# Attention, Fourier mixing and feed-forward on one core: third group's P halves in a weight slot, and VectorE's score operations ordered behind a feed-forward eviction

## The chip, the core and the metric

The kernel runs on one core of a Trainium2 chip. Its engines are TensorE (PE; its weight loads are listed as PEld), VectorE (DVE), ScalarE (ACT), GpSimd (POOL) and SyncE (SP), each with its own instruction stream; they meet only by semaphores. The metric is the device time of one execution in microseconds. Each run gives one time; of several, the median is used.

## What is computed

Eight batches of 576 positions with eight heads of 64 go through causal attention with a window of 128 and a linear bias, then through a two-dimensional Fourier mixing with a residual and a layer norm, then through a feed-forward layer of 512 to 2048 to 512 with a second residual:

```python
scores = np.matmul(q, k.transpose(0, 1, 3, 2)) / np.sqrt(D)
scores = np.where(mask, scores + bias[None], -1e9)      # 0 <= rel < 128
attn = softmax(scores)                                  # exp, sum, divide
x = np.matmul(attn, v).transpose(0, 2, 1, 3).reshape(B, S, H * D)
...
u = x + np.real(np.fft.fft(np.fft.fft(x, axis=1), axis=2))
un = (u - mean(u)) / np.sqrt(var(u) + 1e-06)
return u + np.maximum(un @ w_ch1, 0.0) @ w_ch2
```

Arrays are float32. The kernel multiplies in float16, with most operands split into a high and a low half, so that each product is made of three.

## The kernel before

**Three kinds of work.** Attention goes by pairs of heads, p = 0 to 31, four pairs a batch, two heads e = 0, 1 in each. The transform (`fourier`) and the layer norm of a batch follow its four pairs. The feed-forward (`ffn`) of a batch comes after that: L863 multiplies the first layer into a PSUM tile `fp`, of which there are two; ACT evicts its rectified high half into `hbuf` (L868), and DVE then writes the low half (the lambda behind L868, recorded as L166); L877 multiplies the second layer, again into `fp`, and DVE adds it to X (`X<-fp`, L166). The three kinds run interleaved: while one batch is in attention, earlier ones are in the transform and the feed-forward, so that PE has matmuls of one kind while another waits.

**Attention of pairs 8 to 31.** Each pair's scores come in three groups i = 0, 1, 2, of 384, 512 and 256 columns for each head. PE writes the scores into PSUM tiles `sp`. On DVE `biased` (L456) adds the bias, writes P in float32 and its minimum to `nb`; on ACT the exponential runs in place (`P<-P,nb`, L166). Then `halves` splits P: ACT writes the high half in float16 (L467) and DVE the low half (`P<-P`, L166), both into a second tile, `both`. `flip` (L474) has SP start a transposing DMA of it into `pt`, and PE multiplies `pt` with the values (`pv`, L506, L509, L510).

**Buffers.** The float32 P of `biased` and the halves come from one pool of four buffers named P, for each head one. Which buffer an allocation gets is settled as the program is built. In most groups the halves get the buffers that held the halves of the group before, so ACT's L467 waits there until the transposes that read these have landed; the float32 P mostly gets the other two. `wall` are two constant tiles that hold the feed-forward's weights in nine slots of 1024; half of slot 8 of the second one holds only a small block of zeros at the start.

**What sets the order.** A planner runs pieces of work from a heap by due time: `put(t, f)` for a time, `after(dt, f)` for a delay after the present piece. Groups are numbered n = 3(p - 8) + i; the scores of an even and the following odd n are issued together by `both`, then `biased` of the first group, and `biased` of the second one at its own due time. What the planner emits is then ordered again, engine by engine, by a list scheduler that goes by dependences and buffers; so a new dependence, or another buffer, can move instructions on every engine. Each engine runs its list in order.

**L151** sums squares of q, k and v over the partitions (`total`, `pd<-sq`) for the scales of a later pair; ACT writes these squares at L285.

Of the kernel before, what the change touches and what calls it, by code (L numbers as in the profile page):

```python
# [3 lines left out]

# [6 lines left out]
F32 = mybir.dt.float32  # L11
F16 = mybir.dt.float16
# [4 lines left out]
ALU = mybir.AluOpType  # L17
# [6 lines left out]
NF = 2  # L24
# [11 lines left out]
PB = 4  # L36
# [40 lines left out]
def attn_fft_ffn_kernel(  # L77
# [15 lines left out]
    nc = tc.nc  # L93
    B = q.shape[0]
    V, A, G, T = nc.vector, nc.scalar, nc.gpsimd, nc.tensor
    PSUM = bass.MemoryType.PSUM

    def pool(name, bufs, **kw):
        return ctx.enter_context(tc.tile_pool(name=name, bufs=bufs, **kw))

    const, xp, att = pool("const", 1), pool("xp", 3), pool("att", 2)
# [29 lines left out]
    wall = [const.tile([128, 9, 1024], F32, name=f"wall{i}") for i in range(2)]  # L131
    wf = [t.bitcast(F16).rearrange("p s (e x) -> p s e x", e=2) for t in wall]

    zeros = wall[1][:, 8, 512:576].bitcast(F16)
    G.memset(zeros, 0.0)
    G.memset(wall[1][:, 0], 0.0)

# [27 lines left out]
    def after(dt, f, *a, **kw):  # L165
        put(now[0] + dt, lambda: f(*a, **kw))  # L166
# [3 lines left out]
    behind, marks = [None], {}  # L170
# [272 lines left out]
    def biased(p, i):  # L443
        b, j = divmod(p, 4)
        sp, grp = banks.pop((p, i)), SGRP[i]
        P = Ps[p, i] = {}
        for e in range(2):
            h = 2 * j + e
            nb = small.tile([128, 5], F32, name="nb", bufs=6)
            col = 0  # L450
            whole = P[e] = att.tile([128, 512], F32, name="P", bufs=PB)
            for ti in grp:
                m, n, pc = TILES[ti][1], 128 * len(TILES[ti][2]), PCOL[ti]
                pt = P[e, ti] = whole[:, col:col + n]
                tab, mul = (rel_sb, -2.0 ** -(h + 1)) if b < NF else (psc[p][2], psc[p][1][:m, e:e + 1])
                V.tensor_tensor_reduce(pt[:m, 0:n], sp[e][:m, col:col + n], tab[:m, pc:pc + n],  # L456
                                       mul, 3.0e38, ALU.add, ALU.min, nb[:m, ti:ti + 1])
                after(0.25, A.activation, pt[:m, 0:n], pt[:m, 0:n], AF.Exp, bias=nb[:m, ti:ti + 1], scale=-1.0)
                col += n
            if b >= NF:  # L460
                after(0.45, halves, p, i, e, col)

    def halves(p, i, e, n):
        P32 = Ps[p, i][e][:, 0:n]
        both = att.tile([128, 512], F32, name="P", bufs=PB).bitcast(F16)
        hi, lo = both[:, 0:n], both[:, n:2 * n]
        A.activation(hi, P32, AF.Copy, scale=2.0 ** 14)  # L467
        after(0.2, V.scalar_tensor_tensor, lo, P32, 2.0 ** 14, hi, ALU.mult, ALU.subtract)
        after(0.4, flip, p, i, e, both[:, 0:2 * n])
# [377 lines left out]

    ov = out.rearrange("(t p) d -> t p d", p=128)

    def ffn(b):  # L850
        X = Xs[b]
        parts = [(uTs[b][i], 256, [X[:, XS[2 * i]], X[:, XS[2 * i + 1]]], 4 * b + 2 * i) for i in range(2)]
        if b % 2 == 1:
            parts.append((uTs[b][2], 128, [uts[b // 2]], 4 * B + b // 2))
        for uT, n, tiles, slot in parts:
            per = 512 // n
            hh = []
            for f0 in range(0, 16, per):
                fp = ps_f.tile([128, 512], F32, name="fp")
                for i in range(per):  # L860
                    for c in range(4):
                        for p, (e, j) in enumerate(((0, 0), (0, 1), (1, 0))):
                            T.matmul(fp[:, i * n:(i + 1) * n], w1_ap(e, c, f0 + i), uT[:, j, c, 0:n],  # L863
                                     start=(c == 0 and p == 0), stop=(c == 3 and p == 2))
                    if i == per // 2 - 1:
                        yield
                ht = next(hslots)
                A.activation(ht[:, 0], fp, AF.Relu)  # L868
                after(0.2, V.scalar_tensor_tensor, ht[:, 1], fp, 0.0, ht[:, 0], ALU.max, ALU.subtract)
                for i in range(per):  # L870
                    hh.append(ht[:, :, i * n:(i + 1) * n])
                yield
            for i, t in enumerate(tiles):
                op = ps_f.tile([128, 512], F32, name="fp")
                for f in range(16):
                    for p, (a, e) in enumerate(((0, 0), (0, 1), (1, 0))):
                        T.matmul(op, hh[f][:, a, i * 128:(i + 1) * 128], w2_ap(e, f),  # L877
                                 start=(f == 0 and p == 0), stop=(f == 15 and p == 2))
                    if f % 2 == 1 and f < 15:
                        yield  # L880
                after(0.15, V.scalar_tensor_tensor, t, op, wone, t, ALU.mult, ALU.add)
                after(0.4, nc.sync.dma_start, out=ov[slot + i], in_=t)
                yield
# [4 lines left out]
    for p in range(4 * B):  # L888
        b, j = divmod(p, 4)
# [26 lines left out]
        for i in range(3):  # L916
# [3 lines left out]
            n = 3 * (p - 4 * NF) + i  # L920
# [19 lines left out]
    for b in range(B):  # L940
        t = begin_of(4 * b)
        fourier(b, transform_of(b))
        n = 80 if b % 2 else 64
# [10 lines left out]
    while queue:  # L954
# [6 lines left out]
        for i in fresh:  # L961
            e = i.engine
# [125 lines left out]
```

## Time and profile before

| | us |
|---|---|
| median of three runs | 1046.98 (1043.87 to 1048.29) |
| the profiled execution, its own time | 1043.62 |
| span of its trace | 1041.8 |
| PE busy in the span | 1011.7 |
| DVE busy | 707.2 |
| ACT busy | 551.1 |

The profile lists for every instruction its start, its duration and, in brackets, how long its engine had been idle before it and what ended that idle time. L numbers are lines of the kernel before; L166 is the helper that runs delayed pieces, so several operations of DVE and ACT carry it and are told apart by their tiles. Consecutive matmuls are shown as one row with a count. The granted clock is given as a share of TensorE's full speed.

### The profile page before, as it was taken

The page shows a single profiled execution, that of the slowest core. Times are in us where ns is not written, and L with a number is a line of the kernel's source. Part 1 is how long each engine was busy: PE and PEld are TensorE (multiplying, and loading weights), DVE is VectorE, ACT ScalarE, POOL GpSimd, SP SyncE. Part 2 cuts the span into 40 slices and gives each one's busy share as a digit, 9 for nine tenths or more (in the row PEclk, how much of TensorE's full clock was granted, in tenths as well). Part 3 has the DMA queues.
Part 4 walks back from the last instruction along what each step waited for, and adds up shares of the span by engine and source line. Part 5 has one row for each costly group of instructions (what it writes and reads, how often), then busy time and mean ns, then how long its engine had stood idle before and what let it go on. Part 6 is the DMA issues. An engine that isn't in the chain of part 4 may idle for free.

```text
span 1041.8 us, 23224 instructions
## 1 busy us (share of the span) xinstructions
PE 1011.7 (97%) x9201; PEld 732.2 (70%) x9201; DVE 707.2 (68%) x2124; ACT 551.1 (53%) x1217; POOL 24.2 (2%) x68
## 2 busy tenths in 40 slices
PE   7999999989999999998999999999999999999998
PEld 6978967657676675856585685867586775857756
DVE  5899895977577869796678768698577735351111
ACT  7887865675445755775455654576445521331100
POOL 0000000100000000000000000000000000000000
PEclk9999999999999999999999999999999999999999
DMA  9955223385434543445343543446332510030000
GB/s 359 346 181 163 53 57 95 64 164 110 83 58 98 118 99 81 95 103 117 70 82 70 114 94 69 98 93 143 72 76 45 84 42 11 11 71 2 21 11 21
DMA packets 179789, 97.51 MB, mean 94 GB/s; under 512 B 153952, under 2 KB 162144, under 8 KB 179680
## 3 DMA queue, kind: packets, MB, share of 16 engines
q1 hardware_dynamic: 179392, 95.72, 38.4%
q8 instruction: 72, 1.18, 0.5%
q14 instruction: 37, 0.30, 0.1%
q10 hardware_dynamic: 288, 0.30, 0.1%
HBM read 49.33 MB, written 9.44 MB: 56 GB/s over the span
## 4 chain that ended last, share of the span: by engine, by line
PE 75%; DVE 12%; ACT 5%; DMA 5%; issue 3%; SPq 0%; POOL 0%; ACTq 0%; DVEq 0%; POOLq 0%
PE fp L877 30%; PE fp L863 27%; DMA pt<-P 4%; PE pd L621 3%; PE sp L425 3%; PE sp L427 3%; PE pv L500 3%; DVE P L456 1%; PE sp L483 1%; DVE hbuf L166 1%; ACT P L166 1%; DVE P L166 1%; PE pv L506 1%; PE pd L683 1%; PE pv L509 1%
## 5 line engine op out<-in xcount | busy, mean ns | idle before, releaser
L877 PE MATMUL fp<-wall,hbuf 128*128 128x512 f16 x1728 | 391.3, 379 | 0.1
L863 PEld LDWEIGHTS <-wall 128*128 128x128 f16 x3840 | 340.1, 98 | 57.5 <-issue 12.7
L863 PE MATMUL fp<-uT,wall 128*128 128x256 f16 x3072 | 361.2, 273 | 11.2 <-DVE sc L267 5.2
L877 PEld LDWEIGHTS <-hbuf 128*128 128x128 f16 x1728 | 163.7, 98 | 183.3 <-issue 3.4
L166 ACT ACTIVATE P<-P,nb 128x256 f32<-128x256 f32 x320 | 140.1, 478 | 99.6 <-DVE nb L456 97.5
L868 ACT ACTIVATE hbuf<-fp 128x512 f16<-128x512 f32 x144 | 84.9, 589 | 157.2 <-PE fp L863 157.1
L166 DVE SCALAR_TENSOR_TENSOR hbuf<-fp,hbuf 128x512 f16<-128x512 f32 x144 | 98.9, 688 | 99.8 <-ACT hbuf L868 99.4
L456 DVE CUSTOM_DVE_ANT_0 P<-sp,rg,nsl 128x256 f32<-128x256 f32 x240 | 98.5, 451 | 32.1 <-PE sp L427 29.2
L166 DVE SCALAR_TENSOR_TENSOR P<-P 128x384 f16<-128x384 f32 (+1 forms) x144 | 78.1, 552 | 52.8 <-ACT P L467 52.5
L467 ACT ACTIVATE P<-P 128x384 f16<-128x384 f32 (+1 forms) x144 | 71.8, 515 | 46.3 <-DMA pt<-P 41.8
L166 DVE SCALAR_TENSOR_TENSOR X<-fp,misc,X 128x512 f32<-128x512 f32 x32 | 23.7, 739 | 47.4 <-PE fp L877 47.3
L506 PE MATMUL pv<-vhs,pt 128*128 128x65 f16 x432 | 53.5, 195 | 0.8 <-DVE X L525 0.6
L509 PE MATMUL pv<-vl,pt 128*128 128x64 f16 x432 | 53.5, 193 | 0.0
L510 PE MATMUL pv<-vhs,pt 128*128 128x65 f16 x432 | 53.4, 193 | 0.0
L863 PE MATMUL fp<-wall,wall 128*128 128x128 f16 x768 | 45.8, 219 | 3.3 <-DVE hbuf L166 2.8
L506 PEld LDWEIGHTS <-pt 128*128 128x128 f16 x432 | 41.0, 98 | 8.9 <-issue 1.4
L509 PEld LDWEIGHTS <-pt 128*128 128x128 f16 x432 | 40.3, 99 | 7.4 <-issue 0.2
L427 PE MATMUL sp<-kk,qq 64*128 64x256 f16 x720 | 42.7, 260 | 0.0
L510 PEld LDWEIGHTS <-pt 128*128 128x128 f16 x432 | 40.7, 98 | 0.0
L604 ACT ACTIVATE fh<-abcd,sc 128x512 f16<-128x512 f32 (+1 forms) x21 | 15.1, 719 | 47.9 <-DVE abcd L592 33.2
L427 PEld LDWEIGHTS <-qq 64*128 64x128 f16 x720 | 30.1, 94 | 12.1 <-issue 8.4
L621 PE MATMUL pd<-tab_sb,fh 128*128 128x289 f16 x168 | 37.2, 287 | 0.0
(208 smaller groups left out, 1239.4 us busy)
## 6 DMA issues: line engine op xcount, KB each, us to landing
qr<-q_dram SPq DMA_DIRECT2D x28, 304.0 KB, 3.3
out_dram<-X SPq DMA_DIRECT2D x32, 256.0 KB, 2.3
hbuf<-w_dram SPq DMA_DIRECT2D x16, 511.8 KB, 7.7
vr<-v_dram SPq DMA_DIRECT2D x23, 320.0 KB, 3.1
kr<-k_dram SPq DMA_DIRECT2D x24, 289.0 KB, 2.9
X<-w_dram SPq DMA_DIRECT2D x11, 511.8 KB, 4.0
uT<-w_dram SPq DMA_DIRECT2D x5, 511.8 KB, 4.7
pt<-P SPq DMA_TRANSPOSE x144, 2.9
```

The costliest lines, as they stand in the source:

```text
L166: put(now[0] + dt, lambda: f(*a, **kw))
L425: T.matmul(sp[e][:m, col:col + n], lhs, keys(kk, ti), start=True, stop=True)
L427: o = T.matmul(sp[e][:m, col:col + n], qq[h, c0:c0 + m], keys(kk[h], ti), start=(x == 0), stop=(x == len(prods) - 1))
L456: V.tensor_tensor_reduce(pt[:m, 0:n], sp[e][:m, col:col + n], tab[:m, pc:pc + n], mul, 3.0e38, ALU.add, ALU.min, nb[:m, ti:ti + 1])
L467: A.activation(hi, P32, AF.Copy, scale=2.0 ** 14)
L506: o = T.matmul(pv[:, ti], ph, vh[:, e, vc], start=first, stop=False)
L509: T.matmul(pv[:, ti, 0:D], ph, vl[:, e, vc], start=False, stop=False)
L510: T.matmul(pv[:, ti], pl, vh[:, e, vc], start=False, stop=last)
L621: T.matmul(zp[:, :NS], st["in", c][l][:m, g], tab1_sb[:m, (0 if g < 2 else 2) + t, c], start=(c == 0 and p == 0), stop=(c == 2 and p == 2))
L863: T.matmul(fp[:, i * n:(i + 1) * n], w1_ap(e, c, f0 + i), uT[:, j, c, 0:n], start=(c == 0 and p == 0), stop=(c == 3 and p == 2))
L868: A.activation(ht[:, 0], fp, AF.Relu)
L877: T.matmul(op, hh[f][:, a, i * 128:(i + 1) * 128], w2_ap(e, f), start=(f == 0 and p == 0), stop=(f == 15 and p == 2))
```

## The change

For the third group of a pair (i = 2) `halves` no longer takes a buffer from the pool P, but the second half of slot 8 of the second weight tile, 512 float16 columns for each head. The first and second groups go on taking theirs from the pool. And the first operation of `biased` for a second group (odd n, first head, first tile) now has an order dependence on `marks["fed"]`, the last low-half eviction of the feed-forward's first layer that was emitted before it; a named function, `lower_half`, replaces the lambda, to note that instruction.

```diff
@@ -1,4 +1,4 @@
-from contextlib import ExitStack
+from contextlib import ExitStack, nullcontext
 from heapq import heappop, heappush
 from itertools import count, cycle
 
@@ -132,6 +132,7 @@
     wf = [t.bitcast(F16).rearrange("p s (e x) -> p s e x", e=2) for t in wall]
 
     zeros = wall[1][:, 8, 512:576].bitcast(F16)
+    last_half = wall[1][:, 8, 512:1024].bitcast(F16)
     G.memset(zeros, 0.0)
     G.memset(wall[1][:, 0], 0.0)
 
@@ -453,8 +454,9 @@
                 m, n, pc = TILES[ti][1], 128 * len(TILES[ti][2]), PCOL[ti]
                 pt = P[e, ti] = whole[:, col:col + n]
                 tab, mul = (rel_sb, -2.0 ** -(h + 1)) if b < NF else (psc[p][2], psc[p][1][:m, e:e + 1])
-                V.tensor_tensor_reduce(pt[:m, 0:n], sp[e][:m, col:col + n], tab[:m, pc:pc + n],
-                                       mul, 3.0e38, ALU.add, ALU.min, nb[:m, ti:ti + 1])
+                with tc.issue_after(marks["fed"]) if b >= NF and (3 * p + i) % 2 and e + col == 0 else nullcontext():
+                    V.tensor_tensor_reduce(pt[:m, 0:n], sp[e][:m, col:col + n], tab[:m, pc:pc + n],
+                                           mul, 3.0e38, ALU.add, ALU.min, nb[:m, ti:ti + 1])
                 after(0.25, A.activation, pt[:m, 0:n], pt[:m, 0:n], AF.Exp, bias=nb[:m, ti:ti + 1], scale=-1.0)
                 col += n
             if b >= NF:
@@ -462,7 +464,10 @@
 
     def halves(p, i, e, n):
         P32 = Ps[p, i][e][:, 0:n]
-        both = att.tile([128, 512], F32, name="P", bufs=PB).bitcast(F16)
+        if i == 2:
+            both = last_half[:, 512 * e:512 * e + 512]
+        else:
+            both = att.tile([128, 512], F32, name="P", bufs=PB).bitcast(F16)
         hi, lo = both[:, 0:n], both[:, n:2 * n]
         A.activation(hi, P32, AF.Copy, scale=2.0 ** 14)
         after(0.2, V.scalar_tensor_tensor, lo, P32, 2.0 ** 14, hi, ALU.mult, ALU.subtract)
@@ -847,6 +852,10 @@
 
     ov = out.rearrange("(t p) d -> t p d", p=128)
 
+    def lower_half(ht, fp):
+        V.scalar_tensor_tensor(ht[:, 1], fp, 0.0, ht[:, 0], ALU.max, ALU.subtract)
+        marks["fed"] = nc.cur_bb.bb.instructions[-1]
+
     def ffn(b):
         X = Xs[b]
         parts = [(uTs[b][i], 256, [X[:, XS[2 * i]], X[:, XS[2 * i + 1]]], 4 * b + 2 * i) for i in range(2)]
@@ -866,7 +875,7 @@
                         yield
                 ht = next(hslots)
                 A.activation(ht[:, 0], fp, AF.Relu)
-                after(0.2, V.scalar_tensor_tensor, ht[:, 1], fp, 0.0, ht[:, 0], ALU.max, ALU.subtract)
+                after(0.2, lower_half, ht, fp)
                 for i in range(per):
                     hh.append(ht[:, :, i * n:(i + 1) * n])
                 yield
```

No instruction is added or taken away on the engines; the order of some is other, and so are buffers and waits. In the changed program line numbers are higher: L456 is L458, L467 is L472, L474 is L479, L868 is L877, the low-half eviction is L856 (before: L166), the other delayed pieces are L167, L525 is L530.

On ACT, at the end of pair 19 (470 to 478 us in the trace of before), these are the exponentials, the halves (`P<-P` without `nb`) and the high-half evictions before,

```order
L467 ACTIVATE P<-P 128x512 x2
L166 ACTIVATE P<-P,nb 128x256 x2
L467 ACTIVATE P<-P 128x256
L868 ACTIVATE hbuf<-fp 128x512
L467 ACTIVATE P<-P 128x256
L396 ACTIVATE vhs<-vr,psc 128x10x64
L868 ACTIVATE hbuf<-fp 128x512
```

and after:

```order
L472 ACTIVATE P<-P 128x512 x2
L167 ACTIVATE P<-P,nb 128x256 x2
L472 ACTIVATE wall_106<-P 128x256 x2
L877 ACTIVATE hbuf<-fp 128x512
L397 ACTIVATE vhs<-vr,psc 128x10x64
L877 ACTIVATE hbuf<-fp 128x512
```

The two halves of the third group now write `wall_106` and stand together ahead of the eviction that stood between them.

On DVE, in pair 20 (490 to 498 us), where the second group's scores are first read (ISA is the operation of L456, with a second entry for its minimum; the numbers behind `sp` only tell score tiles apart), before:

```order
L166 SCALAR_TENSOR_TENSOR P<-P 128x384
L456 ISA P,nb<-sp_7099,rg,nsl 128x256
L456 ISA nb 128x1
L456 ISA P,nb<-sp_7099,rg,nsl 128x256
L456 ISA nb 128x1
L166 SCALAR_TENSOR_TENSOR hbuf<-fp,hbuf 128x512
L166 SCALAR_TENSOR_TENSOR P<-P 128x384
L456 ISA P,nb<-sp_7100,rg,nsl 128x256
```

and after:

```order
L167 SCALAR_TENSOR_TENSOR P<-P 128x384
L856 SCALAR_TENSOR_TENSOR hbuf<-fp,hbuf 128x512
L167 SCALAR_TENSOR_TENSOR P<-P 128x384
L856 SCALAR_TENSOR_TENSOR hbuf<-fp,hbuf 128x512
L528 TENSOR_SCALAR ri<-pv,psc 128x5
L529 RECIPROCAL ri<-ri 128x5
L530 TENSOR_TENSOR X<-pv,ri 128x5x64
L856 SCALAR_TENSOR_TENSOR hbuf<-fp,hbuf 128x512
L458 ISA P,nb<-sp_7075,rg,nsl 128x256
L458 ISA nb 128x1
```

The operations of the second group (L456 before, L458 after) moved from ahead of the first of three `hbuf` evictions to behind the third, and behind `ri` and `X<-pv` of pair 19 as well.

On DVE, between pairs 10 and 11 (223 to 228 us), before:

```order
L523 TENSOR_SCALAR ri<-pv,psc 128x5
L524 RECIPROCAL ri<-ri 128x5
L166 SCALAR_TENSOR_TENSOR vl<-vr,psc,vhs 128x640
L525 TENSOR_TENSOR X<-pv,ri 128x5x64
L166 SCALAR_TENSOR_TENSOR X<-fp,misc,X 128x512
L166 SCALAR_TENSOR_TENSOR P<-P 128x256 x2
L456 ISA P,nb<-sp_3022,rg,nsl 128x256
```

and after:

```order
L458 ISA P,nb<-sp_3018,rg,nsl 128x256
L458 ISA nb 128x1
L458 ISA P,nb<-sp_3018,rg,nsl 128x128
L458 ISA nb 128x1
L529 RECIPROCAL ri<-ri 128x5
L167 SCALAR_TENSOR_TENSOR vl<-vr,psc,vhs 128x640
L458 ISA P,nb<-sp_3019,rg,nsl 128x256
L458 ISA nb 128x1
L458 ISA P,nb<-sp_3019,rg,nsl 128x128
L458 ISA nb 128x1
L530 TENSOR_TENSOR X<-pv,ri 128x5x64
L167 SCALAR_TENSOR_TENSOR X<-fp,misc,X 128x512
```

Here the score operations of pair 11 (`sp_3022` and `sp_3023` before, `sp_3018` and `sp_3019` after) moved from behind `X<-fp` and the third group's low halves of pair 10 to ahead of them. In the changed program the P that they write lies in the buffers of the halves of pair 10's second group, and they wait for the transposes of these.

## Rows read from the trace of the kernel before

**Rows 1.** Page, part 1: engine busy us (share of the span) xinstructions

```profile
PE 1011.7 (97%) x9201; PEld 732.2 (70%) x9201; DVE 707.2 (68%) x2124; ACT 551.1 (53%) x1217; POOL 24.2 (2%) x68
```

**Rows 2.** Idle time by releaser: engine line <- releaser: us, times, longest

```profile
ACT P L467 <- DMA pt<-P: 41.8, 29, 3.4
...
PE fp L863 <- DVE hbuf L166: 7.4, 10, 1.9
...
PE fp L863 <- DVE sc L267: 5.2, 2, 3.4
...
PE pd L151 <- ACT wall L285: 3.1, 1, 3.1
...
DVE P L456 <- DMA pt<-P: 2.4, 3, 1.0
...
PE pv L506 <- DVE X L525: 0.6, 1, 0.6
```

**Rows 3.** Groups by line and shape: xcount | busy, mean ns | idle before

```profile
L467 ACT ACTIVATE P<-P 128x512 f16<-128x512 f32 x48 | 29.8, 624 | 14.2 <-DMA pt<-P 13.6
...
L467 ACT ACTIVATE P<-P 128x256 f16<-128x256 f32 x48 | 18.6, 409 | 28.9 <-DMA pt<-P 25.1 <-DVE P L166 2.4 <-DVE nmr L830 1.2
```

**Rows 4.** ACT's timeline, 475 to 477: start, duration (us), instruction [idle before <-releaser]

```profile
475.82 0.42 ACT L467 ACTIVATE P<-P 128x256 f16<-128x256 f32 x1 [3.40 <-DMA pt<-P]
476.14 0.58 ACT L868 ACTIVATE hbuf<-fp 128x512 f16<-128x512 f32 x1
```

**Rows 5.** Timeline of DVE, 476 to 478

```profile
476.27 0.43 DVE L166 SCALAR_TENSOR_TENSOR P<-P 128x256 f16<-128x256 f32 x1 [4.45 <-ACT P L467]
...
477.06 0.67 DVE L166 SCALAR_TENSOR_TENSOR hbuf<-fp,hbuf 128x512 f16<-128x512 f32 x1
```

**Rows 6.** Timeline of PE, 471 to 478

```profile
471.47 1.47 PE L863 MATMUL fp<-uT,wall 128*128 128x256 f16 x12 [0.87 <-DVE X L166]
...
477.79 1.46 PE L863 MATMUL fp<-uT,wall 128*128 128x256 f16 x6 [3.36 <-DVE sc L267]
```

**Rows 7.** Windows: stretch, busy us by engine, granted clock (PEclk), DMA share

```profile
220.00:240.00 20.00, 16.86 (x196) 13.59 (x193) 14.83 (x56) 12.48 (x28) 0.00 (x0) 1.00 0.85 149
275.00:297.00 22.00, 20.79 (x208) 17.81 (x206) 21.70 (x65) 12.79 (x27) 0.62 (x2) 1.00 0.32 74
477.50:481.00 3.50, 3.21 (x16) 2.28 (x17) 2.93 (x11) 3.14 (x8) 0.00 (x0) 0.51 0.48 81
```

**Rows 8.** ACT's timeline at the second such place, 715 to 716

```profile
715.37 0.42 ACT L467 ACTIVATE P<-P 128x256 f16<-128x256 f32 x1 [1.84 <-DMA pt<-P]
```

**Rows 9.** Timeline of DVE, 491.2 to 493, and PE, 492 to 493

```profile
491.30 0.48 DVE L456 CUSTOM_DVE_ANT_0 P<-sp,rg,nsl 128x256 f32<-128x256 f32 x1
...
492.12 0.69 DVE L166 SCALAR_TENSOR_TENSOR hbuf<-fp,hbuf 128x512 f16<-128x512 f32 x1
...
492.86 0.38 PE L863 MATMUL fp<-uT,wall 128*128 128x256 f16 x2 [0.73 <-DVE hbuf L166]
```

**Rows 10.** PE's waits for hbuf's lower half, first and last of eight

```profile
187.14 1.03 PE L863 MATMUL fp<-uT,wall 128*128 128x256 f16 x8 [0.77 <-DVE hbuf L166]
...
734.37 0.81 PE L863 MATMUL fp<-uT,wall 128*128 128x256 f16 x6 [0.81 <-DVE hbuf L166]
```

**Rows 11.** The other two of these waits, at 283 and 344

```profile
283.35 0.81 PE L863 MATMUL fp<-uT,wall 128*128 128x256 f16 x6 [1.10 <-DVE hbuf L166]
...
344.52 0.66 PE L863 MATMUL fp<-wall,wall 128*128 128x128 f16 x9 [1.88 <-DVE hbuf L166]
```

**Rows 12.** ACT, DVE and PE, 224 to 231, around the wait of L151

```profile
226.26 0.42 ACT L467 ACTIVATE P<-P 128x256 f16<-128x256 f32 x1 [2.55 <-DMA pt<-P]
227.15 0.42 ACT L467 ACTIVATE P<-P 128x256 f16<-128x256 f32 x1 [0.47 <-DMA pt<-P]
...
227.94 0.48 DVE L456 CUSTOM_DVE_ANT_0 P<-sp,rg,nsl 128x256 f32<-128x256 f32 x1
...
229.97 0.38 PE L151 MATMUL pd<-sq,misc 128*128 128x3 f32 x2 [3.10 <-ACT wall L285]
```

## Prediction

> **What bounds the kernel now.** I read the page's busy shares first: PE is busy for 1011.7 of 1041.8 us [rows 1], so some 30 us of idle time on PE are all that an edit of orders and waits can win. The view of waits says who ends it [rows 2]: ten waits of L863 for the low half of hbuf (7.4 us), two that it puts down to DVE sc L267 (5.2 us), one of L151 for ACT (3.1 us), one of a value product for X (0.6 us). The first layer has two PSUM tiles; PE stands when neither is evicted, and the eviction is a chain of ACT's high half and DVE's low half. So whatever stands ahead of an eviction on ACT or DVE counts, and only there. The same view has 41.8 us in 29 waits of ACT's L467 for transposes; by shape, 25.1 us fall on the third group (128x256) and 13.6 on the second (128x512) [rows 3]. That is time on ACT; only what reaches an eviction is time of the kernel.
>
> **The wait that sc L267 hides.** At 474 to 478 us three timelines have to be laid side by side. PE stands for 3.36 us until 477.79, just when the low-half eviction on DVE, begun at 477.06, is done [rows 5, 6]; it is this, and not L267, that PE needs. DVE had waited 4.45 us until 476.27, for ACT [rows 5]. ACT stood for 3.40 us at L467, a third group's high half, until a transpose landed, and the high-half eviction is right behind it, at 476.14 [rows 4]. So one wait for a buffer on ACT, not on the data path of the feed-forward, held PE for 3.36 us. At 715 us the same happens with 1.84 us on ACT [rows 8]; that is the other of the two waits of 5.2 us.
>
> **Change, first part: the third group's halves.** Written to a buffer of their own, they wait for their own exponential and for the transposes of the third group of the pair before, whose order on SP is long past. Both big stalls lose their cause. What is late next there is the eviction itself: ACT's 0.58 and DVE's 0.67 us behind the last matmul [rows 4, 5], of which a few tenths stay. I take 0.4 of the 5.2 us as left, a gain of 4.8. [...] Together 6.3 us. Bounds: 3 us if another wait stands ahead of the same evictions, 6.9 if all of it goes.
>
> **Second part: the second group's score operations behind the last eviction.** At 492 us the fault that it removes can be seen: two operations of L456, 0.48 us each, stand on DVE from 491.30 on, ahead of a low half that begins at 492.12, and PE waits 0.73 us for it [rows 9]. Of the ten waits for hbuf two are of another kind (below); the other eight, the first 0.77 and the last 0.81 us [rows 10], sum to 7.4 - 1.10 - 1.88 = 4.4 us. In the changed order the score operations are behind the eviction at all of these but one of about 0.5 us, which has other DVE work ahead of it. Gain 3.8, and 0.6 from the value product's wait [rows 2], and 0.4 of the 0.87 us before X [rows 6], where an L456 stood ahead too: 4.8 us. The price is that this group's exponentials, halves, transposes and value products come later, by 1 to 3 us (three evictions of 0.67 us and some small operations). The next thing that could be late is a transposed P for PE. In the trace of before L467 is the only large waiter for transposes, so the products were early everywhere but at 226 us; I take nothing, with up to 2 us for the range.
>
> **Two stalls that it touches by chance.** At 344 us PE waits 1.88 us for a low half [rows 11]; ahead of that stand the batch's layer norm operations and two L456 on DVE. The new order has some matmuls of the transform earlier, and with them that DVE work, so the eviction is free sooner: 1.4 us, between a gain of 1.9 and a loss of 0.5. At 283 us PE waits 1.10 us [rows 11], but there DVE is busy for 21.70 of 22.00 us [rows 7]: an order can't win what the engine lacks. 0.1 us, with 0 to 1.1 as the bounds.
>
> **What is added: a wait at the head of DVE.** With the third group out of the pool, the first group's P of the next pair gets the buffers of the second group's halves, and has to wait for the transposes of these. In the trace of before the operations of L456 waited for transposes three times only, 2.4 us in all [rows 2]. The place that matters is 223 to 230 us. There two transposes land at 226.2 and 227.1, as the ends of ACT's two waits show [rows 12]. Before, PE lost 3.10 us, in L151, since ACT's squares were behind these two waits. After, L151 stands later in PE's order and this is gone; but the score operations of pair 11, at 227.94 before [rows 12], are now ahead of X<-fp on DVE, and wait for the same two landings. X<-fp is then done near 229.9, PE needs its tile from 226.6 on, and it stands for about 3.3 us; the third group's low halves are behind that, and their transposes come 1 to 2 us too late for the value products. 4.6 instead of 3.1: a loss of 1.5 us, between a gain of 1 (if PE finds other work ahead) and a loss of 4. At the other pair borders the score operations stand at least 4 us behind the landings, counted from the starts of before; only pair 10's second head is as near (0.4 us), and nothing of the feed-forward stands behind it.
>
> The clock has a say here. The 3.10 us of idle time at 227 us left the granted clock at 1.00 [rows 7], the 0.87 and 3.36 us at 470 to 478 did not [rows 6, 7], so I keep no clock term at 227 us. [...]
>
> **The sum.** 6.3 + 4.8 + 1.4 + 0.1 - 1.5 = 11.1 us. On the profiled execution, 1043.6 us, that gives 1032.5. That execution is 3.4 us below the median of the three runs; the median of all four is 1045.4, and 1045.4 - 11.1 = 1034.3. I forecast **1034**.
>
> **Rivals.** First, the waits only change places. VectorE is the busiest engine behind PE, and where it has little idle time the operations put behind an eviction come ahead of the next one; the score tiles in PSUM are also set free later, since it is L456 that reads them, and PE's next scores wait. Then the second part gives nothing, the 1.4 us at 344 us fail, and the first part and the loss at 227 us stay: 6.3 - 1.5 = 4.8 us, about 1040.5. For it speaks the stretch at 283 us; against it that DVE is idle for a third of the span [rows 1] and that stalls of under 1 us are single places.
>
> Second, slower. The wait for the transposes is now on DVE, where the low-half evictions are, instead of on ACT. If at the borders into odd pairs, where both groups' score operations come close together, the landing came after DVE had reached them, each would cost what 227 us cost, 3.1 to 4.6 us. There are 12 such borders; the gains of 6.3 + 4.8 + 1.4 + 0.1 = 12.6 us are eaten up by four of them at the smaller price, and five at a price between, 3.9 us, lose 19.5 us: 7 us slower than before, about 1052. [...] Against it speak the 4 us and more between landings and starts, and that four such borders at once are needed.
>
> Third, the first part doesn't take the wait from ACT but hands it on: the second group's halves still wait for the first group's transposes (13.6 us already [rows 3]), and if these come to stand ahead of the evictions that the third group's did, half of the 6.3 us is lost, and with half of the second part and the loss at 227 us 3.15 + 2.4 - 1.5 = 4 us are left: about 1041.5.
>
> **How the numbers follow.** A measurement of this kernel can tell a difference of about 0.5%, 5.2 us, from none. The forecast, from 1029.5 (each part at its good bound) to 1039, has a chance of 0.66; the first rival, 1039 to 1042, 0.16, half of it past 0.5%; the third, or no gain at all, 1040.5 to 1046, 0.10; the second, slower than before, 0.08, of which 0.06 by more than 0.5%. Faster is 0.66 and half of 0.16, same the other half with 0.10 and 0.02: 0.74, 0.20 and 0.06. The range from 1029 to 1042 reaches half into the third and leaves out some 0.15.
>
> **What would show it.** If the first part is right, the view of waits has no wait of L467's 128x256 form for a transpose any more, the two waits of PE at 474 and 715 us are gone, and so is the half-clock stretch. If the second is, the waits of L863 for hbuf fall from ten to three or four, the one at 283 us among them. The new wait would stand as DVE P L458 <- DMA pt<-P with one entry of 2 to 3 us near 227 us, and PE would wait for X or for a value product there. The prediction is wrong if that row holds many entries with evictions behind them, or if PE's idle time stays near 30 us under other names.

## The result: 0.991 of the time before, by another division of the gain than forecast

The changed kernel took 1034.9 us, the median of five runs (1034.27 to 1037.08); the kernel before took 1043.92 us beside it (five runs, 1040.74 to 1048.29, three of them those of the table of before). The ratio is 0.9914, with a 95% interval from 0.989 to 0.9938. On a second chip it was 0.9933 (0.9914 to 0.9952). The forecast was 1034, within 1029 to 1042, and a gain. The gain was smaller than the 11.1 us of the sum: 9.0 us on the first chip, 6.8 on the second. The forecast time stood on a median of 1045.4 for the kernel before, which further runs brought down.

The profiled execution of after took 1037.08 us, the slowest of its five, with a span of 1034.9 us. Page, part 1, of after:

```profile
PE 1012.4 (98%) x9201; PEld 732.6 (71%) x9201; DVE 707.2 (68%) x2124; ACT 551.6 (53%) x1217; POOL 24.5 (2%) x68
```

PE's idle time is 22.5 us instead of 30.1. PE's busy time, with the same matmuls, is 0.7 us longer, which goes with the mean granted clock, 0.996 here and 0.998 in the trace of before. The view of waits of after, engine, line, releaser, us in all, times, longest:

```profile
ACT P L472 <- DMA pt<-P: 7.6, 6, 2.3
...
DVE P L458 <- DMA pt<-P: 4.5, 2, 3.4
...
PE pv L511 <- DVE X L530: 3.7, 2, 3.4
...
PE fp L872 <- DVE X L167: 3.5, 4, 1.4
PE fp L872 <- DVE hbuf L856: 3.5, 7, 0.8
```

Against [rows 2]: ACT's waits for transposes fell from 41.8 us in 29 to 7.6 in 6; PE's for hbuf from 7.4 in ten to 3.5 in seven, and its two entries under sc L267 (5.2 us) are gone. Longer are PE's waits for X L530, 0.6 us in one before, now 3.7 in two; DVE's waits for transposes, 2.4 us before, now 4.5 with one of 3.4 among them; and PE's waits for X<-fp, 1.3 us in three before, now 3.5 in four. By line and shape (busy, mean ns, idle time ahead), the third group's high half, which writes `wall`, has 0.2 us of idle time ahead of it, against 28.9 us in [rows 3]:

```profile
L472 ACT ACTIVATE P<-P 128x512 f16<-128x512 f32 x48 | 29.8, 624 | 8.1 <-DMA pt<-P 7.6
...
L472 ACT ACTIVATE wall<-P 128x256 f16<-128x256 f32 x48 | 18.3, 402 | 0.2
```

The place at 474 us, in the timelines of ACT, DVE and PE of after; the two halves, the two halves of the eviction and PE follow each other without a hole, and 0.27 us of the 3.36 in [rows 6] are left:

```profile
473.06 0.71 ACT L472 ACTIVATE wall<-P 128x256 f16<-128x256 f32 x2
473.68 0.57 ACT L877 ACTIVATE hbuf<-fp 128x512 f16<-128x512 f32 x1
...
474.30 0.68 DVE L856 SCALAR_TENSOR_TENSOR hbuf<-fp,hbuf 128x512 f16<-128x512 f32 x1
...
475.04 2.14 PE L872 MATMUL fp<-uT,wall 128*128 128x256 f16 x18 [0.27 <-DVE hbuf L856]
```

The place at 223 to 229 us, DVE and PE of after:

```profile
225.89 0.48 DVE L458 CUSTOM_DVE_ANT_0 P<-sp,rg,nsl 128x256 f32<-128x256 f32 x1 [3.44 <-DMA pt<-P]
...
228.11 0.48 DVE L530 TENSOR_TENSOR X<-pv,ri 128x320 f32<-128x320 f32 x1
228.51 0.74 DVE L167 SCALAR_TENSOR_TENSOR X<-fp,misc,X 128x512 f32<-128x512 f32 x1
...
228.74 0.22 PE L511 MATMUL pv<-vhs,pt 128*128 128x65 f16 x1 [3.45 <-DVE X L530]
```

The score operation waits for a transpose until 225.89; X<-pv of the pair before and X<-fp are behind it, and PE waits 3.45 us for the first of these. Windows of after, the granted clock being the third figure from the end:

```profile
228.00:234.00 6.00, 5.26 (x41) 4.13 (x42) 3.54 (x9) 3.91 (x11) 0.00 (x0) 0.50 0.59 158
477.50:481.00 3.50, 3.50 (x43) 3.01 (x42) 1.27 (x6) 1.01 (x4) 0.00 (x0) 1.00 0.57 139
```

The half-clock stretch behind the stall at 474 us [rows 7] is gone; in this execution there is one behind the stall at 225 us, granted at 0.50, and it is twice as long. By windows of 1 us it lasts from 227.8 to 234.6 us; PE works from 228.74 us on. The 24 matmuls of L872 from 229.86 us on took 0.21 us each, 24 of the same at 1.00, from 475.04 us on, 0.11 us each; so the stretch costs an estimated half of 5.9 us, some 2.9 us. In the changed kernel's second profile (below) it is half as long, 3.4 us, with PE at work, and costs 1.7 us by the same estimate. That difference is 1.2 of the 2.2 us by which this execution is above the median; the mean granted clock is 0.996 in this execution and 0.998 in each of the other four.

One of the longer waits for X<-fp is at 707 us in after: on DVE two score operations and X<-fp behind them, and PE.

```profile
706.81 0.48 DVE L458 CUSTOM_DVE_ANT_0 P<-sp,rg,nsl 128x256 f32<-128x256 f32 x1
...
707.21 0.48 DVE L458 CUSTOM_DVE_ANT_0 P<-sp,rg,nsl 128x256 f32<-128x256 f32 x1
...
707.62 0.74 DVE L167 SCALAR_TENSOR_TENSOR X<-fp,misc,X 128x512 f32<-128x512 f32 x1
...
708.41 0.82 PE L872 MATMUL fp<-uT,wall 128*128 128x256 f16 x6 [1.42 <-DVE X L167]
```

### The profile page after: what moved, and what is told of

The parts are those of the page before. It is cut to its first block, busy times and chain, and to the rows that moved or that the text cites. A ratio compares the mean times of both kernels' runs of the same rounds, so it can differ in the third digit from the quotient of the medians.

```text
span 1034.9 us, 23191 instructions
## 1 busy us (share of the span) xinstructions
PE 1012.4 (98%) x9201; PEld 732.6 (71%) x9201; DVE 707.2 (68%) x2124; ACT 551.6 (53%) x1217; POOL 24.5 (2%) x68
## 4 chain that ended last, share of the span: by engine, by line
PE 77%; DVE 13%; ACT 3%; DMA 3%; issue 3%; POOL 0%; SPq 0%; ACTq 0%; DVEq 0%; POOLq 0%
PE fp L872 32%; PE fp L886 28%; PE pd L626 3%; PE sp L428 3%; PE pv L505 3%; PE sp L426 2%; DVE P L458 2%; PE sp L488 1%; DMA pt<-P 1%; PE pd L688 1%; PE pv L511 1%; PE pv L514 1%; PE pv L515 1%; DVE st L828 1%; DVE hbuf L856 1%
## 5 line engine op out<-in xcount | busy, mean ns | idle before, releaser
L872 PEld LDWEIGHTS <-wall 128*128 128x128 f16 x3840 | 340.3, 98 | 49.0 <-issue 9.4
L872 PE MATMUL fp<-uT,wall 128*128 128x256 f16 x3072 | 360.7, 274 | 4.5 <-DVE hbuf L856 2.7
L167 ACT ACTIVATE P<-P,nb 128x256 f32<-128x256 f32 x320 | 140.2, 479 | 110.4 <-DVE nb L458 109.0
L877 ACT ACTIVATE hbuf<-fp 128x512 f16<-128x512 f32 x144 | 85.1, 591 | 179.3 <-PE fp L872 178.9
L856 DVE SCALAR_TENSOR_TENSOR hbuf<-fp,hbuf 128x512 f16<-128x512 f32 x144 | 98.8, 687 | 110.7 <-ACT hbuf L877 110.2
L458 DVE CUSTOM_DVE_ANT_0 P<-sp,rg,nsl 128x256 f32<-128x256 f32 x240 | 96.7, 451 | 32.6 <-PE sp L428 27.8
L167 DVE SCALAR_TENSOR_TENSOR P<-P 128x384 f16<-128x384 f32 (+1 forms) x96 | 58.5, 618 | 16.6 <-ACT P L472 16.1
L472 ACT ACTIVATE P<-P 128x384 f16<-128x384 f32 (+1 forms) x96 | 53.6, 567 | 8.4 <-DMA pt<-P 7.6
L167 DVE SCALAR_TENSOR_TENSOR X<-fp,misc,X 128x512 f32<-128x512 f32 x32 | 23.7, 741 | 46.3 <-PE fp L886 46.3
L872 PE MATMUL fp<-wall,wall 128*128 128x128 f16 x768 | 45.2, 219 | 2.6 <-DVE X L167 1.8
```

Of the source, the lines that this page charges most:

```text
L856: V.scalar_tensor_tensor(ht[:, 1], fp, 0.0, ht[:, 0], ALU.max, ALU.subtract)
```

## Experiments

A word on the times: each comparison is with 7 to 24 runs of the kernel before on the same chip, whose medians were 1041.1 to 1043.5 us; across groups the ratios are compared.

### The whole once more, the parts alone

**The whole.** No edit.

> The changed kernel once more, so that the parts can be compared with the whole on one chip. Expected 0.989 to 0.994 of the kernel before, some 9 us less, with one wait of PE of 3 to 4 us near 225 us and, in some executions, a half-clock stretch behind it.

1036.0 us against 1042.75: 0.9933 (0.9914 to 0.9952), in the expected range; the gain is 6.8 us, where some 9 were expected. PE waits 2.90 us at 226 us, a little less than the 3 to 4 expected, and the half-clock stretch behind it costs 1.7 us.

**Only the first part.**

```diff
-                with tc.issue_after(marks["fed"]) if b >= NF and (3 * p + i) % 2 and e + col == 0 else nullcontext():
-                    V.tensor_tensor_reduce(...)
+                V.tensor_tensor_reduce(...)
```

> Only the first part: the third group's halves in the free half slot, no order behind evictions. By my account the two stalls at 474 and 715 us go (5.2 us, and 1.5 us of half clock), the wait at 225 us comes (3.5 us of idle time and up to 3 us of half clock, against 3.1 us before), and the small stalls of PE for hbuf, 4 us in all, stay: 3 to 5 us below the kernel before. Rival, the waits only change places: the score operations that no longer wait behind ACT come ahead of other evictions, and the time is within 1.5 us of the kernel before.

1047.17 us, 1.0037 (1.0021 to 1.0053): slower by 4.4 us. My account fell here, and the rival's figure was passed on the bad side. The view of waits of this run:

```profile
PE fp L871 <- DVE hbuf L855: 7.1, 8, 2.1
...
DVE P L457 <- DMA pt<-P: 5.4, 3, 2.4
...
PE pv L510 <- DVE X L529: 5.0, 2, 4.0
...
PE pd L152 <- ACT wall L286: 2.2, 1, 2.2
```

The two stalls at 474 and 715 us are gone as expected, but PE's waits for hbuf, 7.1 us, are about as they were (7.4), and there are others: 4.0 of the 5.0 us for X L529 are the place at 225 us, and 2.2 us are a wait of L152 at 581 us for ACT's squares. Each of these two was followed by a half-clock stretch (windows of this run):

```profile
584.50:587.50 3.00, 3.00 (x31) 3.00 (x30) 2.71 (x10) 1.47 (x2) 0.00 (x0) 0.50 0.01 3
229.50:232.50 3.00, 3.00 (x31) 2.45 (x31) 2.12 (x5) 3.00 (x9) 0.00 (x0) 0.50 0.77 235
```

What comes ahead of an eviction is to be seen at 732 us, ACT, DVE and PE of this run:

```profile
731.64 0.63 ACT L471 ACTIVATE P<-P 128x512 f16<-128x512 f32 x1 [1.87 <-DMA pt<-P]
732.18 0.89 ACT L167 ACTIVATE P<-P,nb 128x256 f32<-128x256 f32 x2
732.97 0.57 ACT L876 ACTIVATE hbuf<-fp 128x512 f16<-128x512 f32 x1
...
733.58 0.69 DVE L855 SCALAR_TENSOR_TENSOR hbuf<-fp,hbuf 128x512 f16<-128x512 f32 x1 [0.59 <-ACT hbuf L876]
...
734.33 0.92 PE L871 MATMUL fp<-uT,wall 128*128 128x256 f16 x7 [1.49 <-DVE hbuf L855]
```

The half's wait for the first group's transposes is an old one (the kernel before has 1.82 us there), but two exponentials stand between it and the eviction where one stood, and PE waits 1.49 us, against 0.81 us at the same place in [rows 10]. That fits the rival's account: operations that come sooner come ahead of evictions. The profiled execution is 1.6 us longer than that of before, and shows this much of the 4.4: a second half-clock stretch (1.7 us) with the idle time about unchanged (29.8 us against 30.1). The mean granted clock of every execution tells more. It is 0.9946 over the nine executions of this run and 0.9976 over the 15 of the kernel before beside them; the profiled one, at 0.996, has the second highest of the nine. In the span of 1043.4 us a half-clock stretch of 3.4 us takes 0.0016 off this mean and costs 1.7 us by the estimate above, so the 0.0030 stand for an estimated 3 of the 4.4 us. So the slot alone lost mainly by more half-clock stretches; where the further ones lie, this one profile doesn't show.

**Only the second part.**

```diff
-        if i == 2:
-            both = last_half[:, 512 * e:512 * e + 512]
-        else:
-            both = att.tile([128, 512], F32, name="P", bufs=PB).bitcast(F16)
+        both = att.tile([128, 512], F32, name="P", bufs=PB).bitcast(F16)
```

> Only the second part: score operations of second groups behind the last eviction, halves of all groups in the pool of four. By my account the eight small waits for hbuf go (4 to 5 us less than before) and the two big ones at 474 and 715 us stay, with ACT's waits for transposes at 30 us or more in the 128x256 form. Rival, the order does its work only where ACT is free: the gain is under 1.5 us, since the held operations delay the halves that ACT waits for.

1037.02 us, 0.9946 (0.9924 to 0.9969): 5.7 us less, where 4 to 5 were expected. Waits of PE in this run:

```profile
PE fp L869 <- DVE sc L268: 6.4, 2, 4.8
...
PE fp L869 <- DVE hbuf L853: 4.8, 7, 1.4
```

ACT's half ahead of the worst of them, in its timeline:

```profile
472.65 0.42 ACT L469 ACTIVATE P<-P 128x256 f16<-128x256 f32 x1 [4.33 <-DMA pt<-P]
```

The two big stalls are there, 6.4 us, the first of them longer than before. But the gain came mostly by another way than expected. The small waits for hbuf did not go: of their 4.4 us 3.0 are left, one of 1.36 us at 238 us among them. The largest piece is the wait of L151 at 227 us, 3.1 us in the kernel before, which is gone, since the order of PE's list moved it; another 1.1 us is the wait at 344 us, 0.80 instead of 1.88 us. ACT's waits for transposes fell to 22.8 us, not the 30 that I had expected to be left.

The parts don't add up: +4.4 and -5.7 us alone, -6.8 together. On top of the order the slot is worth 1.0 us here, within the noise of the two runs.

### Taking away the wait that the slot brought in

**Own buffers.** The float32 P and the halves get two buffers each, so that no score operation waits for a transpose (pairs 0 to 7 keep their alternation of four):

```diff
-            whole = P[e] = att.tile([128, 512], F32, name="P", bufs=PB)
+            whole = P[e] = att.tile([128, 512], F32, name="PH" if b < NF and (3 * p + i) % 2 else "P", bufs=2)
...
-            both = att.tile([128, 512], F32, name="P", bufs=PB).bitcast(F16)
+            both = att.tile([128, 512], F32, name="PH", bufs=2).bitcast(F16)
```

> The changed kernel, but the float32 P and the halves have two buffers each of their own instead of four in common, so that a score operation never waits for a transpose; nothing else is edited. If the wait at the head of DVE near 225 us is what holds PE there, it is gone with its half-clock stretch: 3 to 6 us below the changed kernel, and no row DVE P L458 <- DMA pt<-P. Rival, the transposes or the squares of L151 hold PE there anyway: another wait of about 3 us stands near 227 us, and the time is within 1 us of the changed kernel.

1030.48 us, 0.988 (0.9859 to 0.99), 5.5 us below the changed kernel on the same chip, and the best so far. A second run beside another kernel:

> The changed kernel with own buffers once more, to stand beside the next one on the same chip: 0.986 to 0.990 of the kernel before, three waits of PE between 225 and 231 us, 2.4 us in all, behind a second group's half on ACT that waits 4.9 us for a transpose.

1030.87 us, 0.9888 (0.9858 to 0.9918). Waits of the first of the two runs:

```profile
ACT PH L472 <- DMA pt<-PH: 11.8, 7, 4.9
...
PE fp L872 <- DVE hbuf L856: 3.4, 6, 0.8
...
PE fp L872 <- DVE X L167: 3.0, 4, 1.5
```

No row of DVE for transposes is left, and no half-clock stretch. But the wait at 225 us did not go with it: ACT and PE of the same run.

```profile
223.63 0.63 ACT L472 ACTIVATE PH<-P 128x512 f16<-128x512 f32 x1 [4.94 <-DMA pt<-PH]
...
226.63 2.02 PE L872 MATMUL fp<-uT,wall 128*128 128x256 f16 x17 [1.51 <-DVE X L167]
...
229.76 0.38 PE L152 MATMUL pd<-sq,misc 128*128 128x3 f32 x2 [0.47 <-ACT wall L286]
...
231.34 0.20 PE L511 MATMUL pv<-vhs,pt 128*128 128x65 f16 x1 [0.42 <-DMA pt<-wall]
```

Now a second group's half on ACT waits 4.94 us for a transpose, and PE stands 1.51, 0.47 and 0.42 us, 2.4 us in three places instead of 2.90 in one. So the rival was right on the place, though with 2.4 us in three waits and not one of 3, and my account on the time: between the two profiles 0.5 us are idle time there and 1.7 the clock; 0.5 us each lie at 220 and 707 us and 0.8 at 809 us, and 0.8 before 100 us, where the two kernels are alike.

**Is it the buffers, the slot or the order?** The same buffers without one or both of the parts.

> The kernel before, with nothing but the two and two buffers of their own. Control: if the gain of the own buffers is only that they take away the wait that the slot brought in, there is nothing to take away here: within 2 us of the kernel before, the stalls at 474 and 715 us as before. Rival, the buffers themselves are worth something: 4 us or more below the kernel before.

The kernel before with own buffers: 1042.64 us, 0.9993 (0.9977 to 1.0009). No gain that can be told; the buffers are worth nothing by themselves. Of the two stalls only the second is as before; the first is 1.07 us instead of 3.36, and other waits make up for it (PE's idle time is 29.1 us).

> The first part with two buffers each of their own for the float32 P and the halves, and no order behind evictions. The slot alone lost 4 us; the question is to what. If to the wait of the score operations on DVE (the stall near 225 us with its half-clock stretch, and a second one near 581 us), it is gone here: 3 to 6 us below the kernel before. If to the missing order (score operations that come earlier, ahead of evictions), the stalls of PE for hbuf stay at 7 us or so: within 2 us of the kernel before.

Slot and own buffers, no order: 1038.82 us, 0.995 (0.9932 to 0.9968), 4.6 us less. So splitting the pool turns the loss of the slot alone into a gain; the two ratios differ by 0.87%, some 9 us. The order does as much with the common pool (1.0037 against 0.9933), so the loss needs both, the common pool and the missing order. The profiles show 25.1 us of idle time of PE instead of 29.8, and the mean granted clock of the executions is 0.9980 instead of 0.9946. Neither account came out whole: the time is that of the first, but PE's waits for hbuf, 6.4 us, are nearly as they were, as the second had it, and the wait at 225 us is there all the same, again handed to ACT; DVE and PE of this run:

```profile
225.45 0.69 DVE L167 SCALAR_TENSOR_TENSOR PH<-P,PH 128x512 f16<-128x512 f32 x1 [4.78 <-ACT PH L471]
...
227.98 0.48 DVE L529 TENSOR_TENSOR X<-pv,ri 128x320 f32<-128x320 f32 x1
...
228.61 0.19 PE L510 MATMUL pv<-vhs,pt 128*128 128x65 f16 x1 [2.75 <-DVE X L529]
```

> The second part with the own buffers and without the slot. Against the run with slot, order and own buffers (1030.5 us) it gives the worth of the slot by itself. By my account that is the two stalls near 470 and 711 us (4.8 and 1.6 us of idle time) with the half clock behind the first: this run is 6 to 8 us above that one, near the second part alone (1037 us). Rival, most of that gain came from the own buffers: within 2 us of 1030.5 us.

Order and own buffers, no slot: 1041.17 us, 0.9975 (0.9962 to 0.9989), 2.3 us less. The slot, with order and own buffers there, is thus worth 0.988 against 0.9975, some 10 us; I had expected 6 to 8. The two big stalls of PE are in this run:

```profile
PE fp L869 <- DVE sc L268: 6.1, 2, 4.1
```

With a wait of 1.89 us at 224 us and two half-clock stretches (granted at 0.50, an estimated 1.7 us each) these make 11.4 us, where the run with the slot has 2.4 us of waits and none of the stretches. What I can't explain fully is that the order gains 5.7 us with the pool and 2.3 with own buffers; the profiles show 1.7 us more of half clock and the 1.89 us, and that is about the difference.

| slot | order | own buffers | ratio | 95% interval |
|---|---|---|---|---|
| yes | no | no | 1.0037 | 1.0021 to 1.0053 |
| no | yes | no | 0.9946 | 0.9924 to 0.9969 |
| yes | yes | no | 0.9933 | 0.9914 to 0.9952 |
| no | no | yes | 0.9993 | 0.9977 to 1.0009 |
| yes | no | yes | 0.9950 | 0.9932 to 0.9968 |
| no | yes | yes | 0.9975 | 0.9962 to 0.9989 |
| yes | yes | yes | 0.9880 | 0.9859 to 0.9900 |

### The waits for X<-fp

**Order behind the second layer's eviction too**, on top of the own buffers: `marks["fed"]` is also set by X<-fp.

```diff
+    def add(t, op):
+        V.scalar_tensor_tensor(t, op, wone, t, ALU.mult, ALU.add)
+        marks["fed"] = nc.cur_bb.bb.instructions[-1]
...
-                after(0.15, V.scalar_tensor_tensor, t, op, wone, t, ALU.mult, ALU.add)
+                after(0.15, add, t, op)
```

> The changed kernel with own buffers, where the second groups' first score operation also stands behind the last X<-fp emitted, the eviction of the second layer. In the run without this PE waits four times for X, 3.0 us in all. Expected 1 to 2 us below that run (1030.5 us), with the waits of PE for X at 1.5 us or less. Rival, what is held back longer is late elsewhere: the same time within 1 us, with new waits for hbuf or for transposed P.

1030.05 us, 0.9868 (0.9844 to 0.9893): the same as without (0.9880 and 0.9888). PE's waits for X are 3.5 us instead of 3.0. The score operations are gone from ahead of most of them, but what is left is the place at 226 us (1.79 us) and one at 806 us (1.38 us); at 811 us in the changed kernel X<-fp stood behind `vl`, and not behind a score operation. The rival holds on the time; of its new waits only little shows (PE's for hbuf are 3.7 us against 3.4).

### What holds PE at 225 to 232 us

**A third place for halves.** With own buffers, the first head of a second group writes its halves to half a slot of the first weight tile:

```diff
+        elif i == 1 and e == 0 and p > 4 * NF + 1:
+            both = wall[0][:, 8, 0:512].bitcast(F16)
```

> As that one, but the first head of a second group writes its halves to a third place (half a slot of the first weight tile, free from pair 10 on), so that ACT's half near 224 us waits for no transpose. If the cause of what is left at 225 to 231 us is whichever instruction waits for the transposes that land late there, on DVE in the changed kernel, on ACT with own buffers, then the 2.4 us go: 2 to 3 us below it, near 1028 us, with ACT's waits for transposes at 5 us or less in all. Rival, PE is held there by late squares or late value operands in any case: the same time within 1 us, with 2 us of waits between 225 and 231 us.

1031.02 us, 0.9891 (0.9862 to 0.992), the same as its partner. ACT's wait for transposes in the whole run:

```profile
ACT PH L474 <- DMA pt<-PH: 5.4, 4, 1.9
```

PE at that place:

```profile
228.08 0.20 PE L513 MATMUL pv<-vhs,pt 128*128 128x65 f16 x1 [0.71 <-DMA pt<-wall]
...
229.11 0.38 PE L152 MATMUL pd<-sq,misc 128*128 128x3 f32 x2 [0.50 <-ACT wall L286]
...
232.13 0.24 PE L513 MATMUL pv<-vhs,pt 128*128 128x65 f16 x1 [1.85 <-DMA pt<-wall]
```

Now nothing waits for a buffer there, and PE stands 3.06 us for transposes and squares, more than the 2.4 us before. The rival holds: with no buffer to wait for, PE waits for the landing of the transposes itself. In this execution a half-clock stretch of 6.8 us set in during the third of these waits (the mean clock is 0.57 from 230 to 235 us and 0.75 from 235 to 240 us); PE worked in 5.4 us of it, so it cost an estimated 2.7 us.

**Fewer loads.** Two transfers that start near 220 us, pair 12's q and k, are left out; the pair uses pair 11's.

```diff
+        if p == 12:
+            raws[p] = raws[11][:2]
+            return
```

On the changed kernel:

> The changed kernel, but pair 12's q and k are not loaded (two transfers of 304 and 289 KB, which start near 220 us); the pair uses pair 11's, so its values aren't those of the reference. If the transposes land late at 226 us since they share the DMA engines with these loads, the score operations' wait on DVE there falls from 3.4 to 1.5 us or less, and PE's with it: 2 to 4 us below the changed kernel. Rival, the transposes are late because SP issues one after the other, the layer norm's among them, and the loads don't matter: the wait stays at 2.5 us or more.

1033.75 us, 0.9912 (0.9892 to 0.9932), against 0.9914 and 0.9933 with the loads on two other chips: no difference that can be told from the noise, where 2 to 4 us were expected. DVE and PE of this run:

```profile
223.86 0.48 DVE L461 CUSTOM_DVE_ANT_0 P<-sp,rg,nsl 128x256 f32<-128x256 f32 x1 [1.81 <-DMA pt<-P]
...
225.55 0.48 DVE L461 CUSTOM_DVE_ANT_0 P<-sp,rg,nsl 128x256 f32<-128x256 f32 x1 [0.80 <-DMA pt<-P]
...
227.90 2.34 PE L875 MATMUL fp<-uT,wall 128*128 128x256 f16 x20 [2.23 <-DVE X L167]
...
232.38 0.20 PE L514 MATMUL pv<-vhs,pt 128*128 128x65 f16 x1 [0.93 <-DMA pt<-wall]
```

The score operations wait 1.81 and 0.80 us instead of 3.44, and begin at 223.86 instead of 225.89. PE waits 2.23 and 0.93 us, 3.16 in all against 3.45 and 2.90 in the two profiles of the changed kernel, and there is no half-clock stretch. The first wait is between the 1.5 us of the one expectation and the 2.5 us of the other. DVE's list is a little different there, since the program was built anew, so X<-fp and not X<-pv ends PE's wait.

On the kernel with the third place:

> The kernel with own buffers and a third place, with the same two loads left out. There PE waits 3.1 us between 227 and 232 us, 2.6 of it for transposes that have not landed, and no instruction ahead waits for a buffer. If the loads make the transposes late, 2 us or more of the 3.1 go, and the half-clock stretch behind them; if SP's order of issue does, they stay.

1028.6 us, 0.9864 (0.9846 to 0.9882), against 0.9891 (0.9862 to 0.992) with the loads on another chip; the intervals overlap. PE at that place:

```profile
232.14 0.20 PE L516 MATMUL pv<-vhs,pt 128*128 128x65 f16 x1 [1.90 <-DMA pt<-wall]
```

1.90 of the 3.06 us stay, so 1.2 us went, not the 2 expected, and there is no half-clock stretch. So leaving out the loads takes away some of the lateness, 2.0 us at the first landing, and not all of it; in this profile of the changed kernel PE gained the clock by it, and little idle time. But the edit takes away two things at once: the transfers, and their issue on SP. In the timeline of SP the two loads stand right ahead of the transposes in the changed kernel:

```profile
219.99 0.53 SPq L338 DMA_DIRECT2D qr<-q_dram  x1
220.57 0.44 SPq L339 DMA_DIRECT2D kr<-k_dram  x1
221.12 3.72 SPq L479 DMA_TRANSPOSE pt<-P  x2
```

and in the run without them:

```profile
220.31 3.35 SPq L482 DMA_TRANSPOSE pt<-P  x2
```

The transposes are issued 0.8 us sooner there, so up to 0.8 of the 2.0 us may be the order of issue. Whether the rest comes from sharing the DMA engines, and what SP's issuing of one transpose after the other costs (1.2 us or more each in these timelines, the layer norm's among them), was not tried by itself; it stays open.

## Why the prediction was right, and where its steps were not

**What bounds the kernel** held: nothing on PE changed, and the time followed PE's idle time and its clock. The reading of the wait under sc L267 held in full. With the slot, both big stalls went and ACT no longer waited for the third group's transposes; without it, they came back in each run that had the order (6.4 and 6.1 us).

**The first part** (6.3 us) is the step that failed, as a figure that stands by itself. The 4.9 us of idle time at the two stalls went as forecast, but the slot alone was 4.4 us slower, and on top of the order it was worth 1.0 us, where its terms of the sum, 6.3 - 1.5, made 4.8. No run shows the 1.5 us of clock that the 6.3 hold: the trace of before shows the clock at 0.51 from 477.5 to 481 us, with PE at work for 3.21 us of it [rows 7], an estimated 1.6 us, and in the changed kernel that stretch went and another came at 228 us. I priced the new wait of DVE at one place, 227 us, and took the other borders as free, since they had 4 us to spare at the starts of before. Few waits of DVE came there (5.4 us in three with the slot alone). What the working missed is that another use of the pool orders every engine's list anew: more stood ahead of an eviction (732 us), L152 came before ACT's squares were done (581 us), and stalls at new places brought new half-clock stretches, an estimated 3 of the 4.4 us. That the waits only change places was the first rival, but I had it cost the second part and not the first; for the slot alone it took all. With the order and the split pool the slot is worth more than forecast, some 10 us.

**The second part** (4.8 us) had about its size in the run alone, 5.7 us, but that is in part luck: only 1.4 us of it are small waits for hbuf, and 3.1 us are the wait of L151, which the working had counted with the new wait. In the profile of the changed kernel its own terms come to 1.4 us. Of 4.4 us in eight small waits for hbuf 1.4 are left instead of about 0.5; the value product's 0.6 us at 624 us are gone; but PE's waits for X<-fp grew by 2.2 us, a successor that I had priced only as a gain of 0.4 us: at 707 us score operations are ahead of it, at 576 and 811 us other work of DVE, `un` and `vl`. That the transposed P would not be late elsewhere was right.

**The two stalls touched by chance.** 344 us: 1.88 to 0.81 us, a gain of 1.1 where I had 1.4; but it comes from the order and not from the slot, since the run with the slot alone has 2.13 us there and the run with the order alone 0.80. 283 us: 1.10 us became 0.30 and 0.71 us, so 0.1 us gained, as forecast.

**The new wait at the head of DVE** was right in place, cause and size: a landing at 225.9, an entry of 3.4 us, X<-fp done at 229.25 (forecast 229.9), PE idle 3.45 us (forecast 3.3). In place of the 3.10 us of L151 that is a loss of 0.4 us, not the 1.5 of the sum. What it waited for was X<-pv, which stands ahead of X<-fp; and the value products behind were not late by another 1 to 2 us. The clock term that I left out was wrong: the clock was granted at 0.50 there, at a cost of 2.9 us in one execution and 1.7 in the other. I had left it out on a single row of the trace, the one at 1.00 in [rows 7].

**The sum.** In the two profiles PE's idle time fell by 7.6 and 7.7 us; the steps without the clock gave 4.8 + 4.8 + 1.4 + 0.1 - 1.5 = 9.6. In the first profile the second part is 3.4 us short and the new wait 1.1 us better than forecast, which makes the missing 2 us but for a few tenths. The clock, 1.5 us of gain in the sum, was a loss of 1.2 in the first, and gave 0 in the second, since one half-clock stretch came for the one that went. PE's busy time rose by 0.7 and fell by 1.0 us, so in spans the gain is 6.9 and 8.7 us; the medians gave 9.0 and 6.8. That the time came out within 1 us is luck: the gain was 2.1 and 4.3 us smaller than forecast on the two chips, and the start, 1045.4, was 1.5 to 4.3 us higher than the later medians.

## What to carry to other kernels

A wait for a buffer belongs to the pool, not to the instruction: before one user is taken out of a pool, write down who gets its buffers next and what stands behind that one on its engine; here the wait went from ACT, where it delayed evictions, to DVE, where X<-pv and X<-fp stood behind it, and the same four buffers split in two and two gained another 5.5 us. Parts of a change to order and buffers don't add, so time each alone and with its partner before a gain is put down to one. And where a wait comes back under another name after each edit, look for what is late itself; here it was the landing of the transposes, whose own cause is open.

## What the runs showed of the chip that was not expected

The end of the kernel aside, the granted clock fell from 1.00 to 0.50 in ten places of the profiles. In eight of them the stretch was 3.4 us long, with PE at work in nearly all of it, which cost an estimated 1.7 us or a little less; in two it was 6.8 us long, of which PE worked 5.9 and 5.4 us, an estimated cost of 2.9 and 2.7 us. It came in or behind single idle stretches of PE of 1.89, 2.19, 2.75, 2.90, 3.36, 3.45, 3.95, 4.13 and 4.82 us, and once in the third of three in a row, of 0.71, 0.50 and 1.85 us. It did not come with the one of 3.10 us in the kernel before, nor with ten others between 1.87 and 2.23 us. So the length of a wait alone did not tell whether the clock fell.
